# An mLSTM cell and a gated feed-forward layer on one core: the end of the head in another order, short products of zeros, and the last products bank by bank

## The chip, the core and the metric

The program runs on one core of one Trainium2 chip. A core has a matrix engine (TensorE, PE in the profile, with PEld for its weight loads), a vector engine (VectorE, DVE), a scalar engine (ScalarE, ACT), a general engine (GpSimd, POOL) and an engine that here only issues transfers (SyncE, SP). Each works through its own list of instructions in order; they meet through semaphores. The metric is device time in microseconds (us), lower is better. Three runs of the kernel before took 512.22, 512.47 and 513.01 us; the median is 512.47 us.

## The reference

There are 4 x 8 heads (batch B = 4, H = 8) with 768 steps of dimension D = 40. The first block is a recurrence:

```python
for t in range(S):
    m_new = np.maximum(f_gate[:, :, t] + m, i_gate[:, :, t])
    f_stab, i_stab = np.exp(f_gate[:, :, t] + m - m_new), np.exp(i_gate[:, :, t] - m_new)
    C = f_stab * C + i_stab * outer(v_t, k_t)        # D x D state of each head
    n = f_stab * n + i_stab * k_t
    denom = np.maximum(np.abs(n . q_t), 1.0)
    y[:, :, t] = sigmoid(o_gate_t) * (C @ q_t) / denom
```

The result is read as 3072 tokens of 320 numbers, and the second block is

```python
h = x @ w_in          # 3072 x 320 by 320 x 2048
g = h * np.cos(h)
out = g @ w_out       # 2048 x 320
```

All of it is in float32.

## The kernel before

The steps are cut into 6 chunks of 128 (`NC` = 6, `C` = 128). Within a chunk the recurrence is written in its parallel form: a *cell* is one chunk of one batch (24 cells, numbered n = 4c + b), and of each cell the kernel makes the scores `ps` (k times q), multiplies them by a decay matrix `E` (`weigh`), multiplies by v (`values_of`, in the first chunk into a tile `ph`), normalizes (`dn`, `y`), and keeps a state for the next chunk (`seam` into `pu`, `state`). The feed-forward block of chunk c follows one chunk behind: `Up` makes two blocks of 128 of h at a time in two banks `pup`, `near`, `rest`, `sin` and `gate` turn them into g, and the down products add g times w_out into PSUM banks. From chunk 1 on these are Winograd-like: per pair of blocks 12 products, in the last chunk 14, each 128 x 160, into four accumulators `X0, X1, Y0, Y1` of three parts each and, in the last chunk, one more called `late` (the code's L) with two parts. Each part is in its own place in a bank; the output is put together from sums of parts (`combine_first`, `combine`, and the lines at the end of the kernel).

From chunk 1 on most products are issued as *halves*: rows 0 to 63 and rows 64 to 127 of the contraction are two instructions that go to different banks in pairs (`both`, `steps`), and where a bank passes from one half to the other a semaphore of SP orders it (`over`).

The order of the work is written out by hand (`tc.manual_schedule`). The *head* is the four cells of chunk 0 with the loads, gates and weight conversions that belong there. Its order is the string `ORDER`, of which every word is a step in `work`; each step issues its instructions to its engines in that order, so that a word's place decides its place in the list of every engine it uses. The words that matter here: `low4` (four ScalarE copies, line 515, of the dimensions 32 to 39 of q and k of cell 4), `tb4` (two VectorE transposes of q and k of cell 4, line 523), `affine4` (a GpSimd pass over E of cell 4, line 446), `decay4` (eight ScalarE exponentials, line 460), `xT0` to `xT3` and `xL0` to `xL3` (copies of the normalized cells, turned by TensorE in `heads_turn`, into the inputs of the up products), `take`, `cb`, `cj`, `put` 0 to 2 (the conversion of a piece of w_in from 64-bit: ScalarE, VectorE lines 150 and 151, VectorE line 156, GpSimd line 160), `st2` (ScalarE copies of a state), and `ph`, `px`, `pu` (the products of `values_of`, `heads_turn`, `seam`). Behind the head `first_chunk` begins with `Up(0, 0)`: four products of rows 0 to 255 of x (line 802), then `scores(4)` (line 539), then two products of the last 64 rows (line 796), then `weigh(4)` on VectorE, a load of a function table on ScalarE, and the two `near`.

PSUM tiles are handed out in turn (`psum`, `Banks`): in the head the tile of a step takes over the bank of an earlier step, and the first instruction that writes it waits for the readers of that one. So `ph1` takes the bank of the first half of the scores of cell 1, which the second half of `weigh1` reads; `pu3` that of the first half of scores 2; `px1` that of `px0`; `px2` that of the first half of scores 3; `px3` that of `ph3`.

`nil` is a 128 x 128 tile of bfloat16 zeros. Seven products of it (128 x 512) stand at the start of the kernel (line 1057), and two (128 x 384) ahead of the turning of cell 3 (line 677).

At the end, after the 112 products of the last chunk, the outputs of its four batches are put together (lines 960, 965 and 1405 to 1426) and sent: two transfers are issued by SP, two by ScalarE, 160 KB each.

Of the kernel before, what the change touches and what calls it, by code (L numbers as in the profile page):

```python
# [11 lines left out]
FP = mybir.dt.float32  # L12
# [17 lines left out]
def kernel(  # L30
# [20 lines left out]
    nc = tc.nc  # L51
# [495 lines left out]
    def values_of(n, j):  # L547
        if j == 0:
            pool, tag = psum(n)
            heads_of[n] = pool.tile([128, H, D1], FP, name="ph", tag=tag)  # L550
        for p in range(HP):
            h = 2 * p + j
            nc.tensor.matmul(heads_of[n][:, h], Es[n][:, h], vs(n)[:, h, 0:D1], start=True, stop=True)
# [110 lines left out]
    def fade(n):  # L664

        if B <= n < N - B:
            c, b = divmod(n, B)
            for j, r, s, w in halves(n):
                d = tab[r, c, 3, ts(b, H)].rearrange("p (a j) -> p a j", j=2)[:, :, j]
                nc.gpsimd.tensor_tensor(out=s, in0=s, in1=d.unsqueeze(2).to_broadcast([D, HP, w.stop - w.start]), op=OP.mult)  # L670

    def heads_turn(n):
        pool, tag = psum(n)
        px = pool.tile([128, NK + 1, C], FP, name="px", tag=tag)
        if n == B - 1:
            for _ in range(2):
                nc.tensor.matmul(px, nil, nil.unsqueeze(1).to_broadcast([128, NK + 1, 128]), start=True, stop=True)
        for i in range(NK):
            nc.tensor.transpose(px[:, i], ys[n][:, ts(i, 128)], ident)
        for e in range(2):  # L680
            nc.tensor.matmul(px[64 * e:64 * e + 64, NK], ys[n][:, KL:DM], ident, start=True, stop=True)
        pxs[n] = px

    def seam(n):

        if n < N - B:
            pool, tag = psum(n)
            pu = pool.tile([128, HP, DV], FP, name="pu", tag=tag)
            for p in range(HP):
                for j in range(2):  # L690
                    h = 2 * p + j
                    for lo, hi in ((0, 32), (32, D)):
                        nc.tensor.matmul(pu[64 * j + lo:64 * j + hi, p], kws[n][:, h, lo:hi], vs(n)[:, h], start=True, stop=True)  # L693
            pus[n] = pu
# [208 lines left out]
    def products(c, k):  # L903

        S, D1, D4 = Ss[c, k], *(Ds[c][:, k, i] for i in range(2))
        G0, G1 = (gs[c, 2 * k + e].rearrange("q (p e t) -> q p e t", p=2, e=2) for e in range(2))
        B11, T1, B21, B22 = (wv[:, k, e, h] for e in range(2) for h in range(2))
        T2, T3, T4 = (t[:, k] for t in T)
        X0, X1, Y0, Y1 = acc[c]
        made = [(X0, 0, G0[:, 0, 0], B11), (X0, 1, G1[:, 0, 0], B21), (X0, 2, S[:, 0], T2),  # L910
                (Y0, 1, G1[:, 0, 1], T4), (Y0, 0, G0[:, 0, 1], T3), (Y0, 2, S[:, 2], T1)]
        if c == NC - 1:
            made += [(late[c], 0, D1, T1), (late[c], 1, D4, B22)]
        made += [(X1, 0, G0[:, 1, 0], B11), (X1, 1, G1[:, 1, 0], B21), (X1, 2, S[:, 1], T2),
                 (Y1, 1, G1[:, 1, 1], T4), (Y1, 0, G0[:, 1, 1], T3), (Y1, 2, S[:, 3], B22)]
        made = [(bank, bank.tile[:, i], lhs, rhs) for bank, i, lhs, rhs in made]
        if c == 1 and k == 0:
            banks = [bank for bank, *_ in made]
            for j, (_, a, lhs, rhs) in enumerate(made):
                yield a, lhs, rhs, k == 0 and banks[j] not in banks[:j]  # L920
        elif c == NC - 1 and k == LAST:
            x0, y0, L, x1, y1 = made[0:3], made[3:6], made[6:8], made[8:11], made[11:14]
            yield from steps(x0 + L + y1 + x1 + y0, x1 + y0[0:1] + y0[2:3] + y0[1:2] + x0 + L + y1, False, True)
        else:
            ahead = len(made) - 6
            yield from steps(made, made[ahead:] + made[:ahead], k == 0, k == LAST)

    def steps(low, high, first, last):

        issued = [(half, *m) for pair in zip(low, high) for half, m in enumerate(pair)]  # L930
        banks = [m[1] for m in issued]
        for x in range(0, 2 * len(low), 2):
            yield *((*issued[y], first and banks[y] not in banks[:y], last and banks[y] not in banks[y + 1:]) for y in (x, x + 1)), \
                banks[x:x + 2] != banks[x + 2:x + 4]
# [6 lines left out]
    def run(made, n):  # L941
        for _ in range(n):
            now = next(made)
            if len(now) == 3:
                both(*now)
            else:
                a, lhs, rhs, start = now
                nc.tensor.matmul(a, lhs, rhs, start=start, stop=False)

    def all_products(c):  # L950
        acc[c] = [Bank(ps_o.tile([128, 3, HALF], FP, name="acc", tag="o")) for _ in range(4)]
# [61 lines left out]
    def down_slot(c, f2):  # L1013
# [19 lines left out]
        scores1 aff2 pu1 ph0a ph0b weigh11 pu0 weigh10 E30 E31 st0 turnq2 ph1a qT2 lowq0 aff3 maxima dn0 turnk2 st1 y0 kT2  # L1033
        ph1b M1store loads dn1 gexps0 turnq3 qT3 scores2 gexps2 exp2 turnk3 kw3 weigh21 kT3 weigh20 px0 gexpG scores3 pu3 xL0
        ph2a y1 dd exp3 ph2b take0 weigh31 weigh30 st3 ph3a xT0 ph3b cb0 Gstore more_loads px1 dn2 y2 gexps1 gexpW px2 cj0
        take1 xL1 gturn kw2 dn3 xT1 xT2 y3 px3 pu2 take2 gkeep cb1 put0 xT3 cj1 put1 affine4 cb2 low4 xL2 cj2 xL3 put2 tb4
        odd4 qG4 decay4 st2
    """

    def first_cells():  # L1040
# [352 lines left out]
    with tc.manual_schedule():  # L1393
        first_cells()
        first_chunk()
        for c in range(1, NC):
            for b in range(B):
                at_once[0] = (c, b) < (1, 1)
                both_parts(c, b)
        send_kept()  # L1400
        issue(None)
        at_once[0] = True
        run_to(NC - 1, 14 * (LAST + 1))
        for p in range(2):
            combine_first(NC - 1, p)
        L = p2.tile([128, 2, HALF], FP, name="Lc", tag="S")
        nc.scalar.copy(out=L, in_=late[NC - 1].tile)
        for p in range(2):
            combine(NC - 1, p)
        Y0, Y1 = (bank.tile for bank in acc[NC - 1][2:])  # L1410
        o = outs_of[NC - 1, 1]
        tt = nc.vector.tensor_tensor
        tt(out=o[1][:, HALF:DM], in0=Y1[:, 0], in1=o[0][:, HALF:DM], op=OP.add)
        for i in range(2):
            nc.gpsimd.tensor_tensor(out=o[0][:, HALF:DM], in0=L[:, i], in1=o[0][:, HALF:DM], op=OP.add)
        out_to(NC - 1, 2, o[0])
        tt(out=o[1][:, 0:HALF], in0=Y1[:, 1], in1=o[1][:, HALF:DM], op=OP.add)
        tt(out=o[1][:, HALF:DM], in0=late[NC - 1].tile[:, 0], in1=o[1][:, HALF:DM], op=OP.add)
        out_to(NC - 1, 3, o[1], nc.scalar)
        o = outs_of[NC - 1, 0]  # L1420
        tt(out=o[1][:, HALF:DM], in0=Y0[:, 0], in1=o[0][:, HALF:DM], op=OP.add)
        tt(out=o[1].rearrange("q (h n) -> q h n", h=2), in0=Y0[:, 1:3], in1=o[1][:, HALF:DM].unsqueeze(1).to_broadcast([128, 2, HALF]), op=OP.add)
        out_to(NC - 1, 1, o[1])
        tt(out=o[0][:, HALF:DM], in0=Y0[:, 2], in1=o[0][:, HALF:DM], op=OP.add)
        tt(out=o[0][:, HALF:DM], in0=Y1[:, 2], in1=o[0][:, HALF:DM], op=OP.add)
        out_to(NC - 1, 0, o[0], nc.scalar)


# [28 lines left out]
```

## Time and profile before

| | |
|---|---|
| median of three runs | 512.47 us |
| the profiled execution's own time | 509.64 us |
| its span | 507.9 us |
| TensorE busy | 494.5 us, 97% |
| VectorE busy | 405.5 us, 80% |
| ScalarE, GpSimd busy | 286.1 us, 250.8 us |

The span runs from the first to the last instruction of the program; the execution's own time is 1.7 us longer. The profiled execution was 2.8 us shorter than the median of the three runs. The page gives for each engine the time in which it was busy, cuts the span into 40 slices, and lists the costliest groups of instructions with the time the engine sat idle before them and what ended it. Views of the trace give the same for a stretch of time, instruction by instruction: start, duration, engine, line, operation, tiles, shape, number, and in square brackets the idle time ahead and what ended it. A product of float32 appears as two records, a transpose as one. The ends of matrix products are modelled, so that consecutive products overlap in the list.

### The profile page before, as it was taken

The numbers are of one execution on the slowest core, as the hardware profiler recorded it, in microseconds if no ns is written. First come the engines' busy times: TensorE is split into PE (matmuls) and PEld (weight loads), VectorE is DVE, ScalarE is ACT, GpSimd is POOL, SyncE is SP. The second block draws the span as 40 slices with busy tenths as digits, with TensorE's granted clock in tenths as the row PEclk, the third lists the DMA queues.
The fourth block names the chain that finished last, engine by engine and source line by source line (L and its number), as shares of the span: only waits on it lengthen the run. The fifth ranks groups of instructions, "written<-read, shape, count | busy, mean of one in ns | idle before, by whom it ended". The sixth has DMA issues, their size and how long they took to land.

```text
span 507.9 us, 14156 instructions
## 1 busy us (share of the span) xinstructions
PE 494.5 (97%) x5579; PEld 355.0 (70%) x5579; DVE 405.5 (80%) x830; ACT 286.1 (56%) x553; POOL 250.8 (49%) x411
## 2 busy tenths in 40 slices
PE   8898999999999999999999999999999999999995
PEld 6764564646677787776776787677697677777775
DVE  6998999997788787988788898788878778654644
ACT  6778995787843746743747744648635531323230
POOL 8855636467586686346356345355334333121212
PEclk9999999999999999999999999999999999999999
DMA  9987999999803833813822923913842000001001
GB/s 136 185 219 197 238 197 235 225 225 233 172 8 87 165 94 90 162 43 67 211 64 68 204 48 90 214 38 95 188 60 99 2 6 6 1 1 53 1 3 53
DMA packets 97426, 56.95 MB, mean 112 GB/s; under 512 B 62320, under 2 KB 89088, under 8 KB 97360
## 3 DMA queue, kind: packets, MB, share of 16 engines
q1 hardware_dynamic: 95648, 54.28, 48.4%
q0 software_dynamic: 1328, 1.41, 1.2%
q8 instruction: 44, 0.72, 0.6%
q10 hardware_dynamic: 384, 0.36, 0.2%
q14 instruction: 22, 0.18, 0.1%
HBM read 50.69 MB, written 4.10 MB: 108 GB/s over the span
## 4 chain that ended last, share of the span: by engine, by line
PE 81%; DVE 7%; DMA 3%; SPq 3%; ACT 2%; POOL 2%; issue 1%; DVEq 0%; ACTq 0%; POOLq 0%
PE pup L740 33%; PE acc L740 25%; PE late L740 4%; PE pup L802 4%; PE po L841 4%; PE ps L539 3%; PE vt L574 2%; PE vt L565 2%; DMA bits<-in_moe_w_out_dram 1%; SPq L373 1%; PE pup L796 1%; PE pu L693 1%; DMA bits<-in_moe_w_in_dram 1%; DVE n L816 1%; PE vt L571 1%
## 5 line engine op out<-in xcount | busy, mean ns | idle before, releaser
L813 ACT ACTIVATE n<-pup 128x512 int32<-128x512 f32 x96 | 52.2, 593 | 174.4 <-PE pup L740 165.1
L740 PE MATMUL pup<-xT,w_in_sb 64*128 64x512 f32 x608 | 147.9, 595 | 0.2 <-DVE g L825 0.2
L816 DVE SCALAR_TENSOR_TENSOR n<-pup,n 128x512 f32<-128x512 f32 x96 | 61.9, 686 | 71.4 <-ACT n L813 71.3
L896 POOL TENSOR_TENSOR D<-g 128x128 f32<-128x128 f32 x40 | 18.8, 471 | 132.9 <-DVE g L825 124.2
L740 PEld LDWEIGHTS pup<-xT,w_in_sb 64*128 64x128 f32 x608 | 59.1, 187 | 35.6 <-issue 32.8
L821 ACT ACTIVATE n<-n 128x512 f32<-128x512 f32 x96 | 58.7, 629 | 16.2 <-DVE n L816 16.2
L740 PE MATMUL acc<-w_out_sb,g 64*128 64x160 f32 x624 | 63.8, 296 | 0.0
L825 DVE SCALAR_TENSOR_TENSOR g<-pup,n 128x512 f32<-128x512 f32 x96 | 62.1, 681 | 1.4
L740 PE MATMUL acc<-T,g 64*128 64x160 f32 x624 | 61.8, 296 | 0.0
L740 PEld LDWEIGHTS acc<-w_out_sb,g 64*128 64x128 f32 x624 | 55.6, 187 | 8.6 <-issue 8.5
L740 PEld LDWEIGHTS acc<-T,g 64*128 64x128 f32 x624 | 54.2, 187 | 9.7 <-issue 8.9
L460 ACT ACTIVATE E<-E,tab 128x128 f32<-128x128 f32 x160 | 49.0, 388 | 4.2 <-POOL E L446 4.0
L699 POOL DMA_DIRECT2D xL<-xT x38 | 21.2, 560 | 51.6 <-DVE xT L618 40.6
L740 PE MATMUL pup<-xL,w_in_l 64*128 64x512 f32 x152 | 40.2, 589 | 0.0
L740 PE MATMUL acc<-T,S 64*128 64x160 f32 x312 | 39.8, 296 | 0.0
L740 PE MATMUL acc<-w_out_sb,S 64*128 64x160 f32 x312 | 39.4, 296 | 0.0
L841 PE MATMUL po<-w_out_sb,g 128*128 128x320 f32 x128 | 36.9, 440 | 0.9 <-POOL w_out_sb L160 0.9
L802 PE MATMUL pup<-xT,w_in_sb 128*128 128x512 f32 x80 | 37.2, 606 | 0.4 <-DVE g L825 0.3
L841 PEld LDWEIGHTS po<-w_out_sb,g 128*128 128x128 f32 x128 | 23.6, 190 | 13.4 <-POOL w_out_sb L160 4.1
L740 PEld LDWEIGHTS acc<-w_out_sb,S 64*128 64x128 f32 x312 | 30.5, 187 | 3.1 <-issue 3.1
L740 PEld LDWEIGHTS late<-w_out_sb,D 64*128 64x128 f32 x320 | 28.7, 187 | 4.9 <-issue 4.2
L545 DVE TENSOR_TENSOR E<-ps,E 128x512 f32<-128x512 f32 x48 | 30.8, 681 | 1.5 <-PE ps L539 1.3
(198 smaller groups left out, 948.8 us busy)
## 6 DMA issues: line engine op xcount, KB each, us to landing
E<-M_d SPq DMA_DIRECT2D x20, 512.0 KB, 6.7
qr<-in_q_dram SPq DMA_DIRECT2D x34, 160.0 KB, 3.2
kr<-in_k_dram SPq DMA_DIRECT2D x34, 160.0 KB, 3.6
bits<-in_moe_w_out_dram SPq DMA_DIRECT2D x8, 640.0 KB, 6.6
G<-G_d SPq DMA_DIRECT2D x18, 256.0 KB, 6.6
bits<-in_moe_w_in_dram SPq DMA_DIRECT2D x32, 128.0 KB, 5.1
out_dram<-o_sb SPq DMA_DIRECT2D x22, 160.0 KB, 2.8
o<-in_o_gate_dram SPq DMA_DIRECT2D x40, 80.0 KB, 4.0
```

The lines of the kernel that those rows point to most:

```text
L460: nc.scalar.activation(out=Es[n][:, h], in_=Es[n][:, h], func=AF.Exp, scale=-1.0, bias=tab[:, c, 0, g:g + 1])
L539: nc.tensor.matmul(ps[j][:, p], kT[r, p], qT[r, p], start=True, stop=True)
L545: nc.vector.tensor_tensor(out=w, in0=pss[n][j], in1=w, op=OP.mult)
L699: nc.gpsimd.dma_start(out=xL[c][64 * e:64 * e + 64, b], in_=ys[n][0:128:2])
L740: ins = nc.tensor.matmul(a, lhs[r], rhs[r], start=start, stop=stop).ins
L802: nc.tensor.matmul(pu.rearrange("p (b t) -> p b t", b=B), w_in_sb[:, i, ts(part_of(f2, e), 128)], xT[c][:, i:NK * B:NK], start=(i == 0 and ...
L813: nc.scalar.activation(out=self.n[e], in_=self.pu[e], func=AF.Copy, bias=0.25)
L816: nc.vector.scalar_tensor_tensor(out=self.n[e].bitcast(FP), in0=self.pu[e], scalar=0.25, in1=self.n[e], op0=OP.add, op1=OP.subtract)
L821: nc.scalar.activation(out=r, in_=r, func=AF.Sin, scale=TWO_PI_DOWN)
L825: nc.vector.scalar_tensor_tensor(out=g, in0=self.pu[e], scalar=TWO_PI, in1=self.n[e].bitcast(FP), op0=OP.mult, op1=OP.mult)
L841: nc.tensor.matmul(po[c][b], gs[c, f][:, ts(b, C)], w_out_sb[:, f], start=(f == 0), stop=(f == NF - 1))
L896: tt(out=D1, in0=G0[:, 1, 1], in1=G1[:, 1, 1], op=OP.add)
```

## The change

Three places are changed.

- In `ORDER`, `low4` goes ahead of `xL1`; `affine4` between `put0` and `put1`; `tb4` behind `put1`, ahead of `cb2`; `xL3` and `decay4` ahead of `xL2`. On ScalarE the four copies of `low4` so stand ahead of five copies and of `take2` and no longer behind `xT3`; on VectorE the two transposes stand ahead of lines 150, 151, the copy `xL2` and line 156 of the last piece of w_in; on GpSimd the pass over E stands ahead of the second piece's line 160. No transfer is moved.
- `keep_going` issues products of zeros, 128 x 128 each, with their weight load, into the bank that the next step will write: 4, 12, 0 and 4 ahead of `ph0` to `ph3`, 0, 7, 7 and 6 ahead of `px0` to `px3`, 3 ahead of `pu3`. The two of 128 x 384 go. What they write is overwritten.
- The last 14 down products are no longer halves: each is one product over 128 rows, and they come bank by bank: X0 (3), X1 (3), late (2), Y1 (3), Y0 (3). The sums behind them are put in another order on VectorE, GpSimd and ScalarE with two new tiles (`part`, `both`), VectorE has one instruction less, ScalarE has one copy more, and SP issues all four transfers.

```diff
         if j == 0:
             pool, tag = psum(n)
             heads_of[n] = pool.tile([128, H, D1], FP, name="ph", tag=tag)
+            keep_going(heads_of[n].rearrange("q h d -> q (h d)"), (4, 12, 0, 4)[n])
...
+    def keep_going(bank, times):
+        for _ in range(times):
+            nc.tensor.matmul(bank[:, 0:128], nil, nil, start=True, stop=True)
...
-        if n == B - 1:
-            for _ in range(2):
-                nc.tensor.matmul(px, nil, nil.unsqueeze(1).to_broadcast([128, NK + 1, 128]), start=True, stop=True)
+        keep_going(px.rearrange("q i t -> q (i t)"), (0, 7, 7, 6)[n])
...
+            if n == B - 1:
+                keep_going(pu.rearrange("q p d -> q (p d)"), 3)
...
-            yield from steps(x0 + L + y1 + x1 + y0, x1 + y0[0:1] + y0[2:3] + y0[1:2] + x0 + L + y1, False, True)
+            for part in (x0, x1, L, y1, y0):
+                for j, (_, a, lhs, rhs) in enumerate(part):
+                    yield a, lhs, rhs, False, j == len(part) - 1
...
-        take1 xL1 gturn kw2 dn3 xT1 xT2 y3 px3 pu2 take2 gkeep cb1 put0 xT3 cj1 put1 affine4 cb2 low4 xL2 cj2 xL3 put2 tb4
-        odd4 qG4 decay4 st2
+        take1 low4 xL1 gturn kw2 dn3 xT1 xT2 y3 px3 pu2 take2 gkeep cb1 put0 affine4 xT3 cj1 put1 tb4 cb2 xL3 decay4 xL2 cj2
+        put2 odd4 qG4 st2
...
-        tt(out=o[1][:, HALF:DM], in0=Y1[:, 0], in1=o[0][:, HALF:DM], op=OP.add)
-        for i in range(2):
-            nc.gpsimd.tensor_tensor(out=o[0][:, HALF:DM], in0=L[:, i], in1=o[0][:, HALF:DM], op=OP.add)
+        nc.scalar.copy(out=both_of[:, 0], in_=o[0][:, HALF:DM])
+        nc.gpsimd.tensor_tensor(out=both_of[:, 1], in0=L[:, 0], in1=o[0][:, HALF:DM], op=OP.add)
+        nc.gpsimd.tensor_tensor(out=o[0][:, HALF:DM], in0=L[:, 1], in1=both_of[:, 1], op=OP.add)
         out_to(NC - 1, 2, o[0])
-        tt(out=o[1][:, 0:HALF], in0=Y1[:, 1], in1=o[1][:, HALF:DM], op=OP.add)
-        tt(out=o[1][:, HALF:DM], in0=late[NC - 1].tile[:, 0], in1=o[1][:, HALF:DM], op=OP.add)
-        out_to(NC - 1, 3, o[1], nc.scalar)
-        o = outs_of[NC - 1, 0]
-        tt(out=o[1][:, HALF:DM], in0=Y0[:, 0], in1=o[0][:, HALF:DM], op=OP.add)
-        tt(out=o[1].rearrange("q (h n) -> q h n", h=2), in0=Y0[:, 1:3], in1=o[1][:, HALF:DM].unsqueeze(1).to_broadcast([128, 2, HALF]), op=OP.add)
-        out_to(NC - 1, 1, o[1])
-        tt(out=o[0][:, HALF:DM], in0=Y0[:, 2], in1=o[0][:, HALF:DM], op=OP.add)
-        tt(out=o[0][:, HALF:DM], in0=Y1[:, 2], in1=o[0][:, HALF:DM], op=OP.add)
-        out_to(NC - 1, 0, o[0], nc.scalar)
+        tt(out=part, in0=Y1[:, 2], in1=p[0][:, HALF:DM], op=OP.add)
+        tt(out=o[1].rearrange("q (h n) -> q h n", h=2), in0=Y1[:, 0].unsqueeze(1).to_broadcast([128, 2, HALF]), in1=both_of, op=OP.add)
+        tt(out=o[1][:, 0:HALF], in0=Y1[:, 1], in1=o[1][:, 0:HALF], op=OP.add)
+        out_to(NC - 1, 3, o[1])
+        tt(out=p[1][:, HALF:DM], in0=Y0[:, 0], in1=p[0][:, HALF:DM], op=OP.add)
+        tt(out=p[1].rearrange("q (h n) -> q h n", h=2), in0=Y0[:, 1:3], in1=p[1][:, HALF:DM].unsqueeze(1).to_broadcast([128, 2, HALF]), op=OP.add)
+        out_to(NC - 1, 1, p[1])
+        tt(out=p[0][:, HALF:DM], in0=Y0[:, 2], in1=part, op=OP.add)
+        out_to(NC - 1, 0, p[0])
```

(`p` and `o` are the output tiles of batches 0 and 1 and of batches 2 and 3; `tt` is VectorE's addition of two tensors.)

## The prediction

> **What bounds the kernel now.** I read the page's first two parts, then TensorE's waits, then the lists of single instructions of the two places that change, 18 to 50 us and 494 us to the end, and last the granted clock behind the final product.
>
> ```profile
> PE 494.5 (97%) x5579; PEld 355.0 (70%) x5579; DVE 405.5 (80%) x830; ACT 286.1 (56%) x553; POOL 250.8 (49%) x411
> PE   8898999999999999999999999999999999999995
> PEclk9999999999999999999999999999999999999999
> ```
>
> TensorE is the bound from about 110 us to 502 us: from 140 to 495 us its waits come to 0.2 us. What can be won lies ahead of that and behind it. A microsecond won in the head reaches the end only if it moves TensorE's later work, since nothing in between waits.
>
> ```profile
> PE ps L539 <- DVE t L523: 1.3, 1, 1.3
> PE ph L553 <- DVE E L545: 0.8, 1, 0.8
> PE px L679 <- DVE y L644: 0.6, 2, 0.4
> ```
>
> The longest wait of TensorE behind the start is 1.3 us, for the transposes `tb4` ahead of `scores(4)`. Around it, from the lists of VectorE, GpSimd, TensorE and ScalarE:
>
> ```profile
> 34.79 1.33 DVE L151 TENSOR_SCALAR w_in_l<-w_in_l 128x256 int32<-128x256 int32 x1
> 36.24 1.10 DVE L156 SCALAR_TENSOR_TENSOR w_in_l<-low,w_in_l 128x256 int32<-128x256 int32 x1
> 34.69 1.28 POOL L160 TENSOR_TENSOR w_in_sb<-w_in_sb,bits 128x512 int32<-128x512 int32 x1 [2.09 <-DVE w_in_sb L156]
> 35.93 1.15 POOL L446 TENSOR_SCALAR_AFFINE_SELECT E<-E 128x1024 f32<-128x1024 f32 x1
> 39.35 1.16 PE L539 MATMUL ps<-t,t 40*128 40x128 f32 x16 [1.34 <-DVE t L523]
> 41.73 1.09 ACT L813 ACTIVATE n<-pup 128x512 int32<-128x512 f32 x2
> 50.01 0.29 DVE L151 TENSOR_SCALAR w_in_l<-w_in_l 128x256 int32<-128x256 int32 x1
> ```
>
> VectorE's L151 of 128x256 takes 0.29 us at 50.01, where GpSimd is idle, and 1.33 at 34.79, where it ends just behind GpSimd's L160 (35.97). L156 at 36.24 likewise ends 0.27 us behind L446 (37.08). So such VectorE work stands still while GpSimd works; the transposes L523 do not (1.10 and 1.07 us with GpSimd busy beside them).
>
> At the end, from those of ScalarE, VectorE, and the two that issue transfers:
>
> ```profile
> 500.63 0.29 ACT L960 COPY o_sb<-acc 128x160 f32<-128x160 f32 x1 [5.27 <-PE acc L740]
> 502.05 0.33 DVE L1413 TENSOR_TENSOR o_sb<-acc,o_sb 128x160 f32<-128x160 f32 x1
> 504.18 0.32 DVE L1425 TENSOR_TENSOR o_sb<-acc,o_sb 128x160 f32<-128x160 f32 x1
> 503.19 1.71 ACTq L857 DMA_DIRECT2D out_dram<-o_sb  x2
> 503.65 0.83 SPq L340 DMA_DIRECT2D out_dram<-o_sb  x2
> ```
>
> TensorE's last product is modelled to end at 501.96. Seven VectorE steps follow until 504.50, the last transfer is issued at 504.5 and lands 1.9 us later, and 1.5 us on the span ends. The row of the clock, whose last three numbers are the granted clock, the share of the transfers' time and GB/s:
>
> ```profile
> 501.95:505.80 3.85, 0.00 (x1) 0.00 (x0) 2.26 (x8) 0.00 (x0) 1.04 (x2) 1.00 0.43 156
> 505.80:506.20 0.40, 0.00 (x0) 0.00 (x0) 0.00 (x0) 0.00 (x0) 0.00 (x0) 0.50 0.38 138
> ```
>
> It falls to 0.50 only after some 3.8 us without a product; TensorE's idle times in the head are at most 1.34 us.
>
> **The order of the head.** On VectorE the transposes come right behind line 156 of the second piece. GpSimd's `affine4` (1.15 us) now follows `put0` (ends 32.60) and holds VectorE's L150 of that piece, which ran at 32.95, until 33.75: about 0.65 us later. Line 156 ends near 35.2, the transposes run 35.2 to 37.2 beside `put1`, and the last piece then finds GpSimd idle: L150 and L151 0.29 each, the copy 0.28, L156 0.43 (its duration at 75.31), together 1.2 us instead of 2.9. It ends near 38.3, `put2` (0.73) near 39.2, against 38.58 now. So `scores(4)` need not wait: TensorE ends the four products of `Up(0, 0)` at 37.9, does the scores (1.0) and then L796 (1.0) near 39.2 to 40.2 instead of 40.34 to 41.37. ScalarE, whose `near` waited for the table load until 41.73, has `decay4` behind `xT3` instead of behind an idle time of 1.36 us, and is ready near 39.3. So `near` could come 1.5 to 1.65 us earlier, if `Up(0, 0)` still starts at 34.31. `low4` costs nothing: ScalarE does its 1.25 us from 29.8, where it idled 0.30 and 0.71 us; its sources were issued by 25.6 and the two landings that the trace shows are 26.8 and 27.6. What it delays, `xL1`, `xT1`, `xT2` and `take2`, is wanted only at 34.3 and later. E of cell 4, 512 KB, is issued at 27.23 and the v of cell 4, issued behind it on the same queue, landed at 33.63; if E were not there at 32.6, `affine4` would hold `put1`, and with it TensorE, by up to 1.0 us.
>
> **The zeros.** The two old ones of 128x384 start 0.17 us apart (0.50 for both less 0.33 for one); by columns a third of that is 0.058 us, which I take. From above, transposes of 128 columns stand 0.11 apart (four in 0.66); the widest row is 0.17 itself. Ahead of `ph1` twelve zeros do not fill the 0.84 us: they too must wait for VectorE's L545, which reads their bank until 18.17. So `ph1` is 0.7 us late; ScalarE's copies, table load and exponentials behind it carry that to 23.5, where ScalarE idled 0.71, and TensorE takes 0.49 of idle ahead of `px0`; about 0.35 us is left at `scores(3)`. From there all is in TensorE's own line: 3 ahead of `pu3`, 4, 7, 7, 6, that is 27 times 0.058 or 1.55 us, less the idle of 0.44 ahead of `px2` and 0.17 ahead of `px3` and 0.35 of the old zeros: 0.95 with the 0.35. With some 0.2 for changing over to the zeros and back, `Up(0, 0)` starts 1.15 us later, near 35.5. That hides the late `put1` (GpSimd 35.35 to 36.65) but eats most of the gain: `near` comes 1.65 - 1.15 = 0.5 us earlier. Ends: a gain of 1.65 with zeros at no cost; at 0.11 each the delay is 0.35 + 2.97 - 0.96 = 2.4 and the head loses 0.7; at 0.17, 4.0 and a loss of 2.4.
>
> What follows `near` runs on VectorE without a pause to 59.7 us and on TensorE with waits under 0.5 us, so 0.5 us should hold; the transfers wanted next (of 41 to 56 us) are issued in SP's own time, and the closest, a piece of w_out landing at 60.80 for a step at 62.09, leaves room.
>
> The Trainium skill, "TensorE: Matmul & The Clock Gate", Parts 1 and 4, says that the clock is halved after a window of some 3.4 us without enough work, and that transposes do not count as work. By it the stretch of transposes from 29.3 to 34.3 us would halve the clock, `Up(0, 0)` would take 3.6 us longer, and the zeros would win those. This trace does not agree: the clock stays at 1.00 there. What is left of the rule is rival (b).
>
> **The last products.** A whole product costs what two halves do: 24 records of line 948 take 3.26 us (0.136 each, two a product), and the 56 records of the last 14 products 0.068 each, four a product: 0.27 us both ways. They start near 497.95 and end at 501.8 either way. But X0 is done after 3 of 14 instead of 9, X1 after 6 instead of 11, late after 8 instead of 11, Y1 after 11. So the copies, both L965, the copy of late (near 500.7), GpSimd's two (0.52 each, done near 501.95) and `part` fall beside products. Behind Y0 three VectorE steps remain (0.32, 0.49, 0.32), in line behind two with Y1 that wait for GpSimd's first sum (501.4): 501.5 to 502.36. They end near 503.5; SP, at 0.33 to 0.39 an issue, sends the last near 503.65 instead of 504.54: 0.85 us. Should SP's four queue up or GpSimd start 0.5 us late as L1415 did, 0.5; without any wait between, 1.1.
>
> **The sum.** 0.5 + 0.85 = 1.35 us. The profiled execution, 509.64 us by its own time, would be 508.3; set on the median of the runs shown, which is 2.83 us above, 512.47 - 1.35 = 511.1 us.
>
> **The rivals.** (a) Forecast: between -0.7 and -2.3 us, 0.43.
>
> (b) The clock in the timed runs. They are 2.83 us longer than this execution, and I cannot see why. The first seven zeros (128x512) stand 0.42 apart here, twice what 0.17 for 384 columns makes: the clock was half at first, though the row shows 1.00. If in the timed runs it stays half for longer, or falls in the head, the zeros may give back part of the 2.83. All of it: 512.47 - 1.35 - 2.83 = 508.3; half, 509.7. Against: no fall in this trace, and none of the zeros stands before 14 us. 0.18.
>
> (c) The zeros cost as transposes do, 0.11: 0.7 lost in the head, 0.85 won behind: 512.3, no change. With those between: 0.22.
>
> (d) Slower: the zeros stand as far apart as the old ones, 0.17, each held by its weight load (98 ns, and a wait on a bank): 2.4 lost, 0.85 won: 514.0. From 0.115 us a zero on nothing is left. For it: the start of each row of zeros waits for a semaphore; against: two weight loads were issued 0.02 us apart. 0.17.
>
> **How the numbers follow.** About 0.2%, 1.0 us, is what a measurement can tell from no change. Of (a) some 0.39 lies beyond 1.0, of (b) all but 0.01, of (c) 0.03: faster 0.59. (c)'s rest with the near ends of (a) and (d) gives same 0.25, slower 0.16. The range, 509.2 to 513.0, takes in half of (b) and the near half of (d); (a) alone is 510.2 to 511.8.
>
> **What would show it.** `near` of `Up(0, 0)` at 41.2 instead of 41.73, no wait of line 539 on line 523, zeros 0.06 apart, `Up(0, 0)` starting near 35.5; L150/L151 of the last piece at 0.3 us each; the last transfer 1.7 us behind the last product instead of 2.6. It is wrong if the zeros stand 0.1 or more apart, if `put1` holds `Up(0, 0)` because E of cell 4 came late, or if the profiled execution gains what I say and the timed runs gain something else.

## The result, and the profile after

The kernel after took 508.60 us (median of 11 runs, 507.16 to 512.22), the kernel before 512.22 us beside it (11 runs, 510.02 to 513.11): a ratio of 0.9939, 95% interval 0.9917 to 0.9962, 3.6 us. 511.1 was forecast, with a range of 509.2 to 513.0. Three more comparisons of the same two kernels gave 0.9969, 0.9948 and 0.9962 (below); the mean of the four is 0.9955, 2.3 us. So the gain lies between the forecast 1.35 and the 3.6 of the first comparison, whose interval, 1.9 to 4.3 us, takes in the 2.3.

In the profiled executions the difference is smaller. The own time of the one of after is 508.30 us (span 506.3), that of before 509.64 (507.9): 1.34 us, as the sum had it. Its steps do not bear that out. From the page of the kernel after, TensorE's and the other engines' busy times and two rows of slices:

```profile
PE 498.5 (98%) x5592; PEld 359.2 (71%) x5592; DVE 403.8 (80%) x829; ACT 286.2 (57%) x554; POOL 250.3 (49%) x411
PE   9999999999999999999999999999999999999996
PEclk9989999999999999999999999999999999999999
```

The 8 in the third slice of the clock was not there before. By stretches (a row gives start and end, length, each engine's busy time with its number of instructions in the order PE, PEld, DVE, ACT, POOL; the numbers behind the busy times are the granted clock, the transfers' share and GB/s):

```profile
5.91:29.80 23.89, 23.06 (x338) 20.30 (x335) 22.37 (x44) 17.84 (x34) 19.98 (x23) 1.00 1.10 188
29.80:33.21 3.41, 3.41 (x26) 2.56 (x25) 3.27 (x11) 1.94 (x7) 1.67 (x2) 0.50 0.89 183
33.21:50.00 16.79, 16.59 (x193) 9.18 (x193) 13.73 (x24) 14.19 (x35) 9.01 (x11) 1.00 0.97 243
```

In this execution the clock was half for 3.41 us in the head, in spite of the zeros, where the execution of before had full clock all the way to its last product. What that does is seen in TensorE's list, with the `near` of ScalarE below it (start, duration, line, tiles, shapes, number):

```profile
30.13 0.95 PE L675 MATMUL px<-nil 128*128 128x128 bf16 x7
32.07 0.93 PE L675 MATMUL px<-nil 128*128 128x128 bf16 x7
34.72 0.51 PE L675 MATMUL px<-nil 128*128 128x128 bf16 x6
36.39 3.67 PE L807 MATMUL pup<-xT,w_in_sb 128*128 128x512 f32 x8
42.05 1.08 ACT L818 ACTIVATE n<-pup 128x512 int32<-128x512 f32 x2 [1.14 <-PE pup L801]
```

Seven zeros took 0.95 us at half clock, six 0.51 at full. `Up(0, 0)` starts at 36.39, and `near` at 42.05, 0.3 later than before. So this execution won nothing at `near`; its 1.34 us come from the end and from smaller waits between. Two of TensorE's waits in the first 140 us:

```profile
PE ph L675 <- DVE E L545: 0.8, 1, 0.8
PE pup L801 <- DVE g L830: 0.3, 1, 0.3
```

The wait of line 539 on line 523 (1.3 us) is no longer among them, that of the last up products on g went from 0.9 to 0.3. Behind the last product, VectorE's first and last step and SP's issues:

```profile
500.80 0.32 DVE L1426 TENSOR_TENSOR part<-acc,o_sb 128x160 f32<-128x160 f32 x1 [0.54 <-PE acc L955]
502.57 0.31 DVE L1433 TENSOR_TENSOR o_sb<-acc,part 128x160 f32<-128x160 f32 x1
501.64 1.90 SPq L340 DMA_DIRECT2D out_dram<-o_sb  x4
```

The last product is modelled to end at 501.58, VectorE's last step ends at 502.88, 1.3 us behind it instead of 2.55, and the last of SP's four issues begins near 503.2, 1.6 behind the last product.

### The profile page after: what moved, and what is told of

The parts are those of the page before. It is cut to its first block, busy times and chain, and to the rows that moved or that the text cites. A ratio compares the mean times of both kernels' runs of the same rounds, so it can differ in the third digit from the quotient of the medians.

```text
span 506.3 us, 14175 instructions
## 1 busy us (share of the span) xinstructions
PE 498.5 (98%) x5592; PEld 359.2 (71%) x5592; DVE 403.8 (80%) x829; ACT 286.2 (57%) x554; POOL 250.3 (49%) x411
## 4 chain that ended last, share of the span: by engine, by line
PE 87%; DMA 4%; DVE 3%; POOL 2%; SPq 1%; ACT 1%; issue 1%; DVEq 0%; POOLq 0%; ACTq 0%
PE pup L745 33%; PE acc L745 24%; PE po L846 5%; PE pup L807 5%; PE late L745 4%; PE ps L539 4%; PE vt L575 2%; PE vt L566 2%; PE pup L801 2%; DMA bits<-in_moe_w_out_dram 1%; PE acc L955 1%; PE pu L698 1%; DMA bits<-in_moe_w_in_dram 1%; PE vt L569 1%; PE vt L572 1%
## 5 line engine op out<-in xcount | busy, mean ns | idle before, releaser
L745 PE MATMUL acc<-w_out_sb,g 64*128 64x160 f32 x608 | 61.8, 296 | 0.0
L745 PE MATMUL acc<-T,g 64*128 64x160 f32 x608 | 60.0, 296 | 0.0
L745 PEld LDWEIGHTS acc<-w_out_sb,g 64*128 64x128 f32 x608 | 53.8, 187 | 8.6 <-issue 8.5
L745 PEld LDWEIGHTS acc<-T,g 64*128 64x128 f32 x608 | 52.7, 187 | 9.7 <-issue 8.9
L745 PE MATMUL acc<-T,S 64*128 64x160 f32 x304 | 38.5, 296 | 0.0
L745 PE MATMUL acc<-w_out_sb,S 64*128 64x160 f32 x304 | 38.1, 296 | 0.0
L545 DVE TENSOR_TENSOR E<-ps,E 128x512 f32<-128x512 f32 x48 | 30.8, 680 | 2.8 <-PE ps L539 2.6
```

The lines of the kernel that those rows point to most:

```text
L545: nc.vector.tensor_tensor(out=w, in0=pss[n][j], in1=w, op=OP.mult)
L745: ins = nc.tensor.matmul(a, lhs[r], rhs[r], start=start, stop=stop).ins
```

## The experiments

Theory A: the granted clock falls in the head in most runs of the kernel before; the two profiled executions hide that, since before's happened to have no fall and after's happened to have one; the zeros hold the clock up. Rival B: the clock is alike in all runs, and the steps were mis-sized. Each run reports its mean granted clock; half clock for 1 us makes 0.001 of it. The mean also counts half clock behind the last product, which costs no time: the profile of double_order has a mean of 0.996 without a fall in the head. All numbers:

| run | median us | ratio to before, interval | mean clock |
|---|---|---|---|
| before_again | 510.76 | 0.9990, 0.9970 to 1.0011 | 0.9918 |
| zeros_only | 510.24 | 0.9987, 0.9968 to 1.0005 | 0.9968 |
| no_zeros | 510.33 | 0.9987, 0.9971 to 1.0003 | 0.9918 |
| tail_only | 510.15 | 0.9978, 0.9956 to 1.0001 | 0.9925 |
| after_again | 509.41 | 0.9969, 0.9943 to 0.9994 | 0.9971 |
| order_only | 512.06 | 1.0010, 0.9986 to 1.0033 | 0.9887 |
| head_only | 510.96 | 0.9989, 0.9964 to 1.0013 | 0.9962 |
| narrow_zeros | 512.17 | 1.0009, 0.9982 to 1.0036 | 0.9877 |
| after_third | 508.61 | 0.9948, 0.9931 to 0.9965 | 0.9981 |
| zeros_early | 510.29 | 0.9984, 0.9965 to 1.0003 | 0.9932 |
| zeros_late | 510.09 | 0.9981, 0.9963 to 1.0000 | 0.9927 |
| double_zeros | 508.86 | 0.9953, 0.9935 to 0.9971 | 0.9993 |
| double_tail | 510.52 | 0.9956, 0.9937 to 0.9976 | 0.9988 |
| double_order | 511.07 | 0.9971, 0.9952 to 0.9989 | 0.9980 |
| mid_zeros | 508.93 | 0.9941, 0.9918 to 0.9964 | 0.9975 |
| double_early | 508.98 | 0.9934, 0.9912 to 0.9956 | 0.9991 |
| after_fourth | 509.10 | 0.9962, 0.9940 to 0.9985 | 0.9980 |
| pause | 508.19 | 0.9939, 0.9915 to 0.9963 | 0.9987 |

The kernel before itself stood at 0.989 to 0.991 in all these comparisons (median 510.89 to 512.22). Rows 1 to 4, 5 to 8, 9 to 12, 13 to 16 and the last two were each run on one chip, beside the kernel before; from one such group to another the ratios are to be compared, not the medians. The kernel after has 43 short zeros (the expectations count 47), double_zeros 86 (94), mid_zeros 63 (69), double_early and pause 66.

**Does the clock fall, and do the zeros hold it?** The kernel before once more, and its parts.

> The kernel before once more, unchanged, for the granted clock of each of its runs. Theory A (the clock): the runs of the kernel before lose 2 to 3 us because TensorE's clock is half for some microseconds of the head. Then the mean granted clock of most runs is below the 0.998 of the profiled execution, by about 0.001 for each microsecond at half clock (1 us of 508 at 0.50), and the runs with the lower clock are the longer ones; median 512.2. Theory B (the steps): the clock is the same in all runs, and what differs is when transfers and engines are done; clocks of 0.998 throughout, whether a run takes 510 or 513.

> The kernel before with the short zeros alone (the two long ones gone, as in the change). Theory A: the zeros keep the clock up, the runs gain 1.5 to 2.5 us: 510.2, ratio 0.996, with a higher mean clock than the kernel before. Theory B: the zeros only take TensorE's time, 1.1 us of it ahead of Up(0,0), of which the idle time of 1.3 us ahead of scores(4) takes up most: 512.2 to 512.8, ratio 1.000 to 1.001.

> The kernel after without the short zeros (the two long ones stand again, order and tail as changed). Theory A: the clock falls in the head as in the kernel before, and it gains only what the profile gives, 1.35 to 2.7 us (order 0.5 to 1.6, tail 0.85 to 1.1): 509.5 to 510.9, that is 1 to 2.3 us slower than the kernel after, ratio 0.9945 to 0.9975, with a lower clock. Theory B: without the zeros Up(0,0) starts 1.2 to 2 us earlier, and it is as fast as the kernel after or faster: 507.5 to 508.6, ratio 0.991 to 0.993.

> The kernel before with the last 14 products whole and bank by bank, and the sums and transfers behind them as in the change; head as before. Both theories: 0.85 to 1.1 us gained, 511.1 to 511.4, ratio 0.998. If it is 2 us or more, neither holds and the end is what was mis-sized.

zeros_only is the change without its first and third part (the two old products of 128x384 go here too):

```diff
+            keep_going(heads_of[n].rearrange("q h d -> q (h d)"), (4, 12, 0, 4)[n])
...
+        keep_going(px.rearrange("q i t -> q (i t)"), (0, 7, 7, 6)[n])
...
+            if n == B - 1:
+                keep_going(pu.rearrange("q p d -> q (p d)"), 3)
```

no_zeros is the kernel after with these lines taken out again (and the two old products of 128x384 put back); tail_only is the kernel before with the lines of the last 14 products and of the end alone:

```diff
-            yield from steps(x0 + L + y1 + x1 + y0, x1 + y0[0:1] + y0[2:3] + y0[1:2] + x0 + L + y1, False, True)
+            for part in (x0, x1, L, y1, y0):
+                for j, (_, a, lhs, rhs) in enumerate(part):
+                    yield a, lhs, rhs, False, j == len(part) - 1
...
```

The new profile of the unchanged kernel before, by stretches, and its first `near`:

```profile
6.12:19.78 13.66, 12.52 (x194) 10.98 (x193) 12.62 (x19) 8.97 (x18) 10.64 (x12) 1.00 1.24 157
19.78:26.60 6.82, 6.82 (x42) 5.93 (x40) 5.42 (x14) 3.49 (x5) 5.55 (x6) 0.50 1.04 236
26.60:45.00 18.40, 16.69 (x217) 11.19 (x216) 15.61 (x33) 14.86 (x42) 11.94 (x14) 1.00 0.77 207
44.06 1.09 ACT L813 ACTIVATE n<-pup 128x512 int32<-128x512 f32 x2
```

The same kernel that had 1.00 throughout now has 6.82 us at half clock. Its `near` of `Up(0, 0)` starts at 44.06 instead of 41.73. TensorE's products, 0.34 us later than in the first profile at 18 us, are 2.33 later at 34 us, and 1.59 of that is left at 490 us. Mean clocks: 0.9918 here and without zeros, 0.9925 with the end alone, 0.9968 with the zeros. That is A; B, which had 0.998 everywhere, falls. A's sizes did not all hold: zeros alone won 0.7 us (interval -0.3 to 1.6) and not 1.5 to 2.5. The wait ahead of `scores(4)`, which the new order removes, is still there (TensorE's waits in zeros_only):

```profile
PE ps L539 <- DVE t L523: 1.1, 1, 1.1
```

It is no longer than the 1.3 of before, so that it does not show where the rest went; this stays open. And no_zeros won 0.7 us where 1.35 or more was expected. The end alone gave 1.1 us by ratio (interval 0 to 2.2).

**The whole again, the head by its parts, and zeros of 16 columns.**

> The kernel after once more, unchanged, beside the kernel before on one chip, for the clock of each run. Theory A (the zeros hold the clock up): the mean clock of its runs is 0.996 to 0.998 where the kernel before has 0.990 to 0.992, and it is 3 to 3.6 us faster, ratio 0.993 to 0.994. Theory B (the parts add up as single parts did, zeros 0.8 and tail 1.0): 1.8 us faster, ratio 0.9965.

> The kernel before with the new order of the head alone. By the forecast's own step, without the zeros the four scores products come 1.3 us earlier: 0.5 to 1.65 us gained, ratio 0.997 to 0.999. Theory A: TensorE's work then stands in the same clock as before, and the clock takes part of it back: 0 to 0.6 us, ratio 0.999 to 1.000, mean clock 0.990 to 0.992.

> The new order and the zeros, the end of the kernel as before. Theory A: order and zeros need each other, since zeros alone fill up into the wait ahead of scores(4): 2 to 2.5 us gained, ratio 0.995 to 0.996, mean clock 0.996 to 0.998. Theory B: the zeros alone gave 0.8 and the order nothing: 0.8 us, ratio 0.9985.

> The kernel after with each zero product 16 columns wide instead of 128, as many of them, in the same places, each with its weight load. If they stand about as far apart as the wide ones (0.055 us, set by the weight load), TensorE's times are the same and only the streamed columns are fewer. Theory A with the clock following the streamed columns: the clock falls as without zeros, 0.991 to 0.993, and 1.5 to 2 us of the gain are lost, ratio 0.997. If the clock follows that TensorE has something to do at all: as the kernel after, ratio 0.993 to 0.994, clock 0.996 or more. If they stand 0.02 us apart, the head is shorter by up to 1.6 us and only the clock tells.

order_only is the kernel before with the new `ORDER` alone, head_only has the lines of zeros_only besides:

```diff
-        take1 xL1 gturn kw2 dn3 xT1 xT2 y3 px3 pu2 take2 gkeep cb1 put0 xT3 cj1 put1 affine4 cb2 low4 xL2 cj2 xL3 put2 tb4
-        odd4 qG4 decay4 st2
+        take1 low4 xL1 gturn kw2 dn3 xT1 xT2 y3 px3 pu2 take2 gkeep cb1 put0 affine4 xT3 cj1 put1 tb4 cb2 xL3 decay4 xL2 cj2
+        put2 odd4 qG4 st2
```

narrow_zeros is the kernel after with

```diff
-            nc.tensor.matmul(bank[:, 0:128], nil, nil, start=True, stop=True)
+            nc.tensor.matmul(bank[:, 0:16], nil, nil[:, 0:16], start=True, stop=True)
```

The zeros ahead of `ph1` in TensorE's list, narrow_zeros first, then after_again:

```profile
18.50 0.46 PE L675 MATMUL ph<-nil 128*128 128x16 bf16 x12 [0.78 <-DVE E L545]
```

```profile
18.35 0.84 PE L675 MATMUL ph<-nil 128*128 128x128 bf16 x12 [0.24 <-DVE E L545]
```

and narrow_zeros by stretches:

```profile
21.08:24.50 3.42, 3.42 (x24) 2.87 (x24) 3.10 (x13) 2.25 (x2) 3.32 (x6) 0.50 0.88 243
24.50:31.32 6.82, 6.68 (x104) 6.06 (x103) 5.96 (x15) 6.30 (x14) 4.50 (x5) 1.00 0.77 210
31.32:41.56 10.24, 10.24 (x82) 5.85 (x81) 8.12 (x18) 7.75 (x26) 5.60 (x6) 0.50 0.89 228
```

Twelve narrow zeros stand (0.46 - 0.17) / 11 = 0.026 us apart, the wide ones (0.84 - 0.23) / 11 = 0.055. As many instructions in the same places with the same weight loads, at half the time on TensorE, leave the clock at 0.9877 and cost 2.8 us against after_again (by the means 2.3, standard error 0.7). So it is what the products stream that holds the clock, not that TensorE has an instruction. This is the clearest run for A: it removes the cost and keeps the form, and is slower.

Two stretches of 3.41 us show it at close range, both filled by products of 41 columns with zeros between them, and both without idle time on TensorE. In narrow_zeros 26 records of 41 columns, one transpose and eleven narrow zeros start in it, in after_fourth 26 such records and nine wide zeros; narrow_zeros first:

```profile
27.91:31.32 3.41, 3.41 (x41) 3.41 (x41) 3.27 (x8) 3.35 (x10) 2.17 (x2) 1.00 0.92 241
```

```profile
27.00:30.41 3.41, 3.41 (x38) 3.41 (x37) 3.29 (x8) 3.35 (x10) 2.24 (x2) 1.00 0.84 219
```

The first is followed by the 10.24 us at half clock, the second by full clock to the end of the products.

The whole again had the clock that A said, 0.9971, but not its time: it won 1.6 us (interval 0.3 to 2.9), beside 3 to 3.6 by A and 1.8 by adding up the parts. The order alone won nothing (0.5 slower, within its interval): its profile has two stretches at half clock, 6.83 and 3.41 us. head_only, at 0.9962, won 0.6 where 2 to 2.5 were expected; in its profile TensorE is 0.79 us ahead of before at 83 us and 0.28 behind at 105 us; its waits between 84 and 128 us come to 2.6 us, before's to 1.1.

**Which zeros, and how many.**

> The kernel after unchanged, on the chip of the next three, to set the size of the gain: two comparisons gave a ratio of 0.9939 and 0.9969. Expected between them, 0.9955, 2.3 us; mean clock 0.996 to 0.998.

> The kernel after with the zeros ahead of ph0, ph1, ph3 and pu3 alone (23), none ahead of px1 to px3. Theory A says which falls they prevent: those of 19 to 26 us do not come, those of 31 to 38 us do. Mean clock 0.993 to 0.995, halfway between 0.991 and 0.997; 1.2 us of TensorE's time saved against it: 0 to 1 us slower than the kernel after. Rival: only the zeros ahead of the turning matter (most falls lie there): clock 0.991, 1.5 us slower.

> The kernel after with the zeros ahead of px1 to px3 alone (20). Theory A: the falls of 31 to 38 us do not come, those of 19 to 26 us do. Mean clock 0.993 to 0.995; 0 to 1 us slower than the kernel after. Rival, as above: clock 0.996 or more and as fast as the kernel after or up to 0.5 us faster, since ph1 no longer waits with its zeros.

> The kernel after with twice as many zeros in every place (94 instead of 47), to see the price of zeros where the clock has nothing left to gain. Theory A: mean clock 0.998 or 0.999; 47 more at 0.055 us are 2.6 us of TensorE's time, nothing of it in waits but some 0.5: Up(0,0) 2 us later in the profile and 1 to 1.7 us slower than the kernel after, less 0.5 from the falls that are left. Rival: the clock is at its limit by chance and not for want of columns: the same clock as the kernel after.

zeros_early is the kernel after with

```diff
-        keep_going(px.rearrange("q i t -> q (i t)"), (0, 7, 7, 6)[n])
+        keep_going(px.rearrange("q i t -> q (i t)"), (0, 0, 0, 0)[n])
```

zeros_late has `(0, 0, 0, 0)` for `(4, 12, 0, 4)` and 0 for the 3 of `pu3`; double_zeros has `(8, 24, 0, 8)`, `(0, 14, 14, 12)` and 6.

Both halves are needed: 0.9932 and 0.9927, between 0.9902 and 0.9981, and each 1.5 to 1.7 us slower than the whole, more than the 0 to 1 expected; the rivals (one half does it all) fall. zeros_early has its fall at 34.97, behind the turning that has lost its zeros; the profile of zeros_late has none, so that what its half leaves open is seen in the mean clock alone. Twice as many hold the clock in every run (0.999 or 1.000), and then six runs lie between 508.80 and 508.97, where those of the kernel before spread over 3.5 us. The 43 more cost 0.25 us in the median and not 1 to 1.7: at full clock `Up(0, 0)` starts at 36.84 instead of 34.74 to 35.56, but runs that lost a stretch to the clock are gone. Over all profiles, the clock falls in the head in five of the six without wide short zeros, in one of the two with half of them, and in one of the twelve with all 43 or more.

**What order and end are worth when the clock holds.**

> Doubled zeros and the new end, the order of the head as before: with the clock held up, runs scatter by 0.1 us instead of 1, so that the difference to the doubled zeros with both changes (508.86) is the worth of the new order alone. The forecast's step: order won 1.65 at near without zeros, and 0.5 to 1.1 with more zeros in front: 509.4 to 510.0. Rival: what is won at near is given back in the waits of 53 to 126 us on w_out and g: 508.8 to 509.1. By the run of the order alone (0.4 slower): 508.4.

> Doubled zeros and the new order, the end as before: the difference to 508.86 is the worth of the new end. The forecast's 0.85: 509.7. By the lists of single instructions (2.6 us from the last product to VectorE's last end before, 1.3 after) 1.2 to 1.3: 510.1.

> The kernel after with half as many zeros more in every place (69 instead of 47). Theory A with a threshold of work in each stretch of 3.4 us: if 69 are above it too, the runs stand as close together as with 94 and the head is 1.3 us shorter than there, of which 0.5 to 1 reaches the end: 507.9 to 508.4, mean clock 0.999, faster than both kernels. If not: scatter of 0.5 to 1 us around 508.6 and some clocks of 0.994 to 0.997.

> The zeros ahead of ph0, ph1, ph3 and pu3 doubled, those ahead of px1 to px3 as in the kernel after (66). It tells where the falls left in the kernel after come from: if from the stretch of the ph products (the profile of the kernel after has its fall behind them, at 29.8 us), the clock is 0.999 in all runs and the time 508.0 to 508.5; if from the turning, as the kernel after: 0.996 to 0.998, 508.6 with a scatter of 1 us.

mid_zeros is the kernel after with

```diff
-            keep_going(heads_of[n].rearrange("q h d -> q (h d)"), (4, 12, 0, 4)[n])
+            keep_going(heads_of[n].rearrange("q h d -> q (h d)"), (6, 18, 0, 6)[n])
...
-        keep_going(px.rearrange("q i t -> q (i t)"), (0, 7, 7, 6)[n])
+        keep_going(px.rearrange("q i t -> q (i t)"), (0, 10, 10, 9)[n])
```

and 4 ahead of `pu3`; double_early has `(8, 24, 0, 8)`, `(0, 7, 7, 6)` and 6.

double_tail is double_zeros with the old `ORDER`, double_order is double_zeros with the old lines of the last products and the end. They ran on another chip than double_zeros. By the medians order would be worth 1.7 us and the end 2.2, too much for both; by the ratios 0.15 and 0.9, each uncertain by more than 1 us. The runs are not as quiet as expected (509.05 to 510.76, 509.43 to 511.55). The traces show one reason. From 42 to 83 us double_zeros and double_order agree to 0.03 us; VectorE and GpSimd behind that, double_zeros first, then double_order with what TensorE waits for:

```profile
83.13 0.17 DVE L594 TENSOR_SCALAR dn<-dt 128x8 f32<-128x8 f32 x1
83.34 0.94 DVE L595 SCALAR_TENSOR_TENSOR dn<-dt,dn 128x8 f32<-128x8 f32 x1
83.16 1.10 POOL L446 TENSOR_SCALAR_AFFINE_SELECT E<-E 128x1024 f32<-128x1024 f32 x1
```

```profile
83.14 1.10 DVE L594 TENSOR_SCALAR dn<-dt 128x8 f32<-128x8 f32 x1
84.28 0.98 DVE L595 SCALAR_TENSOR_TENSOR dn<-dt,dn 128x8 f32<-128x8 f32 x1
83.13 1.08 POOL L446 TENSOR_SCALAR_AFFINE_SELECT E<-E 128x1024 f32<-128x1024 f32 x1
86.20 1.69 PE L801 MATMUL pup<-xL,w_in_l 64*128 64x512 f32 x4 [0.81 <-DVE g L830]
```

Where GpSimd's pass starts 0.023 us behind VectorE's step of 128 x 8, the step takes 0.17; where it starts 0.011 ahead, the step stands still to its end, and TensorE waits 0.81 for g. In the 18 profiles up to here the step took 0.17 eleven times (GpSimd 0.013 or more behind, or later altogether) and 1.09 to 1.12 seven times (from 0.022 ahead to 0.009 behind). A second such place at 105 us adds 0.4 (TensorE's work is 0.98 later in double_order at 95 us, 1.39 at 110 us). Taking this out (TensorE's work at 180 us is 1.39 later in double_order, its end 2.32) the end is worth 0.93 us. The same reading of tail_only against before (its last up product 2.68 later, its end 1.69) gives 0.99, of the kernel after against head_only (0.86 earlier, its end 1.85 earlier) 0.99. For the order, double_tail reaches the up products at 57 us 0.62 later than double_zeros; how much of that is left at the end is not shown.

mid_zeros and double_early are faster than before by 0.6 to 0.7% but not shown to be faster than the kernel after; both have runs above 511. Whether the falls left come from the ph products or the turning stays open.

**Without the race at 83 us.**

> The kernel after unchanged, as the measure for the next: ratio 0.994 to 0.997, 508.6 to 509.4, scatter 1 us.

> The kernel with the zeros ahead of ph0, ph1, ph3 and pu3 doubled (66), and GpSimd held back by short fills of an unused tile (128x128, 2 of them at the first place, 5 at the second) ahead of the pass L446 over E in the two turns at about 82 and 104 us. In the profiles VectorE's step of 128x8 (tensor_scalar into dn) takes 0.17 us where L446 starts 0.013 us or more behind it, and 1.09 to 1.12 where it starts before that: 7 of 18 profiles; TensorE then waits 0.9 us for g. Theory C (a race of some 10 ns between the two engines is what is left of the scatter): with L446 0.4 us later at the first place the step takes 0.17 in every run, and at the second 0.17 instead of 0.5 to 0.85; 508.0 to 508.4, scatter 0.5 us, below the kernel after by 0.3 to 0.6. Rival: the fills hold VectorE as L446 does, or what is late on GpSimd is missed later: 508.6 to 509.5.

pause is double_early with

```diff
+    pause = const.tile([128, 128], FP, name="pause")
...
+            for _ in range(2 + 3 * x):
+                nc.gpsimd.memset(pause, 0.0)
             decay_exponents(m + 2)
```

```profile
82.19 0.46 POOL L1278 MEMSET pause<- 128x128 f32 x2
82.18 0.23 DVE L594 TENSOR_SCALAR dn<-dt 128x8 f32<-128x8 f32 x1
82.45 0.17 DVE L595 SCALAR_TENSOR_TENSOR dn<-dt,dn 128x8 f32<-128x8 f32 x1
84.92 1.35 DVE L606 TENSOR_TENSOR so<-og,dn 128x128 f32<-128x128 f32 x1
```

The step takes 0.23, the next 0.17 instead of 0.94, the step at the second place 0.17, and six runs lie between 508.03 and 508.87, beside after_fourth's 507.10 to 512.37 on the same chip: by the means 508.29 against 509.40, 1.1 us with a standard error of 0.48. C holds for the step, in one profile. That the time and the smaller scatter come from it is not shown: pause has 66 zeros too, and double_early, with the same 66 and no fills, stands at a ratio of 0.9934 beside 0.9939, six of its seven runs between 507.96 and 509.11 and one at 512.39. Its profile shows a price at L606 (1.35 instead of 0.28), which GpSimd's later work now holds: TensorE waits 1.9 us for line 619 between 84 and 128 us, and its last product ends at 502.05, in double_early at 501.19.

## Why the prediction was wrong, point by point

**The step that failed** is the one that set rival (b), the clock, aside ("Against: no fall in this trace") and had the zeros as a cost alone; the 1.35 was then taken from a median 2.83 us above the profiled execution. The reason given was that the clock falls only after some 3.8 us without a product, read from the end of that trace, while TensorE's idle times in the head are at most 1.34 us. The runs show falls without that: the one in before_again follows 3.41 us with 1.14 us idle, the one in after 3.41 us with none, and behind the last product of after the clock fell after 2.7 us. So the prediction's own last sign of being wrong is what came: the profiled execution gained what it said, and the timed runs something else. The profiled execution of before was one of the few without a fall in the head: of 140 runs of the kernel before in these comparisons 15 have a mean clock of 0.997 or more, of 43 runs of the kernel after 33. By that:

| | before | after | difference |
|---|---|---|---|
| clock 0.997 and above | 510.10 (15 runs) | 508.85 (33) | 1.25, standard error 0.30 |
| all | 511.44 (140) | 509.18 (43) | 2.26, standard error 0.24 |

At about full clock the change is worth the forecast 1.35 within its error; by the difference of the rows another 1.0 us comes from runs that no longer fall to half clock. The bound is rough, since the mean also counts the end of the program: from 0.998 on it is 1.04 us with a standard error of 0.52, from 7 and 27 runs. The zeros stood in the sum as 1.15 us at `Up(0, 0)`; the term missing from the sum is about -1.0 on the mean run, and zeros_only, which has that term and the cost together, won 0.7. That, and a first comparison that by scatter came out 1.3 us above the mean of four, make 3.6 of 1.35. The 0.18 for (b) was too low, and half of it, a gain of 2.8, is nearer to the 2.3 than the forecast. That 1.35 fits at full clock is in part luck: both of its terms were too small (below), and waits behind `near` took some back.

**The clock's windows.** The prediction weighed that the turning would halve the clock and held the trace against it. In other profiles falls do stand behind the turning, at 31.50 us (tail_only), 34.66 (no_zeros), 36.29 (order_only) and 34.97 (zeros_early); earlier ones, at 19.22 to 21.08 us (order_only, before_again, narrow_zeros), stand behind TensorE's wait ahead of `ph1`. In all 20 profiles every change of the clock lies at a whole number of 3.41 us from the first rise, as 23.89 (7) in the profile of after, 13.66 (4) and 20.48 (6) in that of before_again, 17.07 (5) in narrow_zeros, 30.72 (9) in zeros_early. The Trainium skill, "TensorE: Matmul & The Clock Gate", Part 1, says that the clock is decided in free-running windows of 3413 ns, so that one kernel meets them differently in each execution. The rows agree with that. What Part 4 of that page in the Trainium skill says, that transposes do not count as work, no run here shows: no such window holds transposes alone, and the stretch that the prediction took for them has products too (lines 681 and 693).

**The zeros' price.** 0.058 apart forecast, 0.055 measured; `ph1`'s twelve wait for L545 as said. `Up(0, 0)` near 35.5: 34.74, 35.56 and 35.39 in three profiles of the kernel after without a fall. Rivals (c) and (d) fall.

**`near` at 41.2.** In those three 40.88, 41.48 and 41.32, though their first scores started 0.13, 0.58 and 0.41 us later than before's. Counted from there the head wins 0.82 to 0.98 us, more than 0.5; the order of VectorE and GpSimd did what was said (L150 and L151 of the last piece 0.27 to 0.29, no wait on L523). Two details came otherwise: in two of the three GpSimd's pass over E held line 645 (1.1 us) and not L150, and in after_again the pass waited 0.89 us for its transfer, so that `put1` held `Up(0, 0)` by 0.21, the sign of being wrong that the prediction named, at a small size.

**"0.5 us should hold"** behind `near` does not always: after_again, 0.84 ahead of before at 55 us, is 1.2 behind it at 127 us, having waited in between for pieces of w_out (1.4 us in all) and for g (1.6). The waits named as roomy are not.

**The end.** 0.85 forecast, 0.93 to 0.99 measured: 0.1 too little, and within the ends given.

## What to carry to other kernels

One profiled execution shows one draw of the clock: read the granted clock of every run before setting a sum on the median, and where the timed runs lie well above the profiled one, look there first. Short products of zeros ahead of products that stream little were worth more here than the TensorE time they take, and only wide ones: 128 columns held the clock, 16 did not. A part measured alone can lose its gain to the clock that another part holds up, so compare parts where the clock is full.

## What the runs showed of the hardware that was not expected

- At full clock the six runs of double_zeros stand within 0.2 us. Full clock alone does not do it: the eight runs of double_order, at 0.996 to 0.999, spread over 2.1 us. The kernel before, mostly with half clock somewhere in the head, spreads over 3 to 6 us in each comparison.
- TensorE can be without a pause and still lose its clock: in the 3.41 us ahead of the fall in the profile of after it had no idle time, with 29 records of products of 41 columns and four zeros, while 26 such records and nine zeros kept it in after_fourth. How much it takes to hold the clock these runs do not give: of two stretches with 0.44 us idle and nearly the same records, before's from 27.92 us kept the clock and tail_only's from 28.08 us lost it.
- 10 ns between the starts of two engines decide over 0.94 us: VectorE's 128 x 8 step takes 0.17 us where GpSimd's pass over E starts 0.013 us or more behind it, and 1.1 where that starts from 0.022 ahead to 0.009 behind. A GpSimd fill in that place let it pass in 0.23. The Trainium skill, "SBUF — State Buffer", section "Who interferes with whom", says of a VectorE instruction in a mode that takes both port pairs that the one who issues first has the shared ports for the whole instruction, and the other blocks fully. These rows agree where GpSimd is first; where VectorE is first, GpSimd's pass is only some 0.025 us longer (1.104 to 1.113 against 1.082 to 1.086), and whether the step runs in such a mode no run here shows.
